# Attention scores on quarters of the TensorE array, with a PSUM bank per head

## The chip, the cores and the metric

The kernel runs on one core of one Trainium2 chip. A core has five engines that work on their own queues and wait for each other through semaphores: TensorE (PE in the profile; its weight loads are listed as PEld), VectorE (DVE), ScalarE (ACT), GpSimd (POOL) and SyncE (SP), which here issues nearly all DMA transfers. Matmuls write to PSUM, eight banks of 128 partitions by 512 fp32 words; everything else is in SBUF. The metric is the device time of one execution in microseconds (us). Before the change the median of three runs is 691.74 us (691.67 to 692.97).

## The reference

Two stages, all in fp32. The inputs q, k and v have 4 batches, 8 heads, 768 positions and 64 dimensions.

```python
k_sum = k.reshape(B, H, nb, 32, D).max(axis=3)          # nb = 24 summaries per head
v_sum = v.reshape(B, H, nb, 32, D).mean(axis=3)
scores_l = scale * q @ k.T                               # kept where |i - j| < 16
scores_s = scale * q @ k_sum.T + log(32)
a = softmax over [scores_l masked, scores_s]
attn = a @ [v, v_sum]                                    # (B, H, S, D)
x = attn.transpose(0, 2, 1, 3).reshape(B * S, H * D)     # 3072 x 512
h = x @ w_in                                             # 3072 x 2048
out = (h * erf(softplus(h))) @ w_out                     # 3072 x 512
```

So each query sees at most 31 neighbours and 24 summaries. The second stage, two large matrix products, is most of the arithmetic.

## The kernel before, in words

The work is cut into 12 chunks of 256 positions (3 per batch). In a chunk, attention is done in four "quads", one per pair of heads (`NP = 4`; quad number `qd = 4 * chunk + pair`), 48 in all. A quad has four blocks of 64 queries (`NB = 4`). The keys that a block can see are a window of 96, and with the 24 summaries each block has `NK = 120` columns of scores.

The scores of a quad (`scores`, L232 to L246) use a block diagonal. The tile `qb` holds, for each of the four blocks, a 128 x 128 matrix with the first head's queries in its upper left quarter and the second head's in its lower right; the other quarters are zero, cleared once by GpSimd (L57, L75). `load_quad` fills the two diagonal quarters with two transfers from `q_t` (L209). The keys of both heads lie one above the other on 128 partitions (`kw`, or `kfirst` and `ksum` for the first four quads). One matmul per block gives 128 rows (2 heads x 64 queries) by 120 columns, so four matmuls fill 480 columns of one PSUM bank. An fp32 matmul appears in the profile as two instructions.

What follows for a quad: `maxima` adds the mask out of PSUM (L254, DVE) and takes the row maximum (L257, L260); `exps` (L271, ACT); `weights_of` divides by the sum (DVE, L277 to L281); `transp` turns the weights, four PE transposes into PSUM (L291); `tcopy` copies them to SBUF as `pt` (L297, ACT); `av` multiplies by the values (L308, 8 matmuls of 64 output rows); `xsplit` takes the result out of PSUM as a high part xh and a rest xl (L326 or L328, and L329).

All these small PSUM results share the pool `ps_a`: two banks, taken in turn by `scores`, `transp`, `av` and the summaries' transpose (`summaries_turn`, L161). The hidden layer (`mm1`, L342) has the four banks of `ps_h` and the output (`mm2`, L395) the two of `ps_o`. The scores of the first four quads use a bank of `ps_h` each, and their q lies in `qbs` and `qfirst`.

The hidden layer goes in steps: 12 chunks by 4 groups of 512 hidden units, 48 steps k. Matrices are in a split form (a high and a low part, three passes) from the second chunk on; for the first chunk they are used in full fp32, and DVE puts each weight group together from raw words (`to32`, L106, L108, L110) while ACT and DVE then make the high and low parts (`high`, L127; `low`, L135).

The order of each engine's instructions is the order in which the program is written (`manual_schedule`); there is no planner. Up to step 3 the order is spelled out line by line (L446 to L611): this is the run-up. From k = 4 a loop (L613) does the same in each round: scores of quad k + 5, `mm1` first half, transposes of quad k + 4, `mm1` second half, `av` of quad k + 4, `mm2` of step k - 1. Steps 45 to 47 are written out again. Within a queue an instruction that waits holds up all that stands behind it.

Of the kernel before, what the change touches and what calls it, by code (L numbers as in the profile page):

```python
# [9 lines left out]
F32 = mybir.dt.float32  # L10
# [4 lines left out]
ALU = mybir.AluOpType  # L15
AX = mybir.AxisListType
PSUM = bass.MemoryType.PSUM
# [4 lines left out]
NP = H // 2  # L22
NTH = 3
NB = 4
NS = 24
LW = 96
NK = LW + NS
T = 256
# [12 lines left out]
def block_attention_mlp(ctx: ExitStack, tc: tile.TileContext, q_t, k_nat, k_win, v_tok, v_nat, v_win, w_in, w_out, out):  # L41
    nc = tc.nc

    const = ctx.enter_context(tc.tile_pool(name="const", bufs=1))
    wts = ctx.enter_context(tc.tile_pool(name="wts", bufs=1))
    two = ctx.enter_context(tc.tile_pool(name="two", bufs=2))
    one = ctx.enter_context(tc.tile_pool(name="one", bufs=1))
    small = ctx.enter_context(tc.tile_pool(name="small", bufs=2))
    ps_h = ctx.enter_context(tc.tile_pool(name="ps_h", bufs=4, space=PSUM))
    ps_o = ctx.enter_context(tc.tile_pool(name="ps_o", bufs=2, space=PSUM))  # L50
    ps_a = ctx.enter_context(tc.tile_pool(name="ps_a", bufs=2, space=PSUM))

# [7 lines left out]
    mask_sb = const.tile([128, 5, NK], F32, name="mask_sb")  # L60
    nc.gpsimd.memset(mask_sb[:, :, 0:LW], 0.0)
    nc.gpsimd.memset(mask_sb[:, :, LW:NK], 8.0 * math.log(32.0))
    for a in range(2):
        m = mask_sb[64 * a:64 * a + 64, :, 0:LW]
        nc.gpsimd.affine_select(out=m, in_=m, pattern=[[0, 5], [1, LW]], compare_op=ALU.is_ge, fill=-8e9, base=-1, channel_multiplier=-1)
        nc.gpsimd.affine_select(out=m, in_=m, pattern=[[0, 5], [-1, LW]], compare_op=ALU.is_ge, fill=-8e9, base=31, channel_multiplier=1)
    nc.gpsimd.memset(mask_sb[:, 0, 0:16], -8e9)
    nc.gpsimd.memset(mask_sb[:, 4, 80:LW], -8e9)
# [44 lines left out]
    def weave(*gens):  # L113

        gens = list(gens)
        while gens:
            for x in list(gens):
                if next(x, x) is x:
                    gens.remove(x)
# [37 lines left out]
        nc.vector.tensor_reduce(vs_sum[:, LW:NK], vn.rearrange("d (n w) -> d n w", n=NS), op=ALU.add, axis=AX.X)  # L157

    def summaries_turn(b, p):
        tp = ps_a.tile([128, 512], F32, name="pa")  # L160
        nc.tensor.transpose(tp[0:NK, 0:128], vs_sum, ident)  # L161
        nc.scalar.mul(vsum[b % 2][LW:NK, p], tp[LW:NK, 0:128], 1.0 / 32.0)

    kfirst = {}
# [36 lines left out]

    def load_quad(qd, values=True):
        ch, b, th, p = where(qd)
        qb = qbs[qd % 2] if qd not in qfirst else qfirst[qd]
        first = qd < NP
        kw = None if first else two.tile([128, NB, NK], F32, name="kw")
        for a in range(2):
            r = slice(64 * a, 64 * a + 64)
            nc.sync.dma_start(out=qb[r, :, r], in_=q_t[b, p, r, th * T:(th + 1) * T].rearrange("d (j q) -> d j q", j=NB))  # L209
# [12 lines left out]
    def ksum_quad(qd):  # L222
        ch, b, th, p = where(qd)
        s = st[qd]
        nc.gpsimd.tensor_copy(s["kw"][:, :, LW:NK], ksum[b % 2][:, p:p + 1, :].to_broadcast([128, NB, NS]))
# [4 lines left out]
        nc.sync.dma_start(out=s["vw"][LW:NK], in_=vsum[b % 2][LW:NK, p:p + 1, :].to_broadcast([NS, NB, 128]))  # L230

    def scores(qd):  # L232
        s = st[qd]
        sc = ps_h.tile([128, 512], F32, name="sf", tag="hps") if qd < NP else ps_a.tile([128, 512], F32, name="pa")
        for j in range(NB):
            if qd >= NP:
                parts = [(0, s["kw"][:, j])]
            else:

                kn, k0 = kfirst[qd], 64 * j - 16  # L240
                parts = [(0, kn[:, k0:k0 + LW])] if j else [(0, kn[:, 0:16]), (16, kn[:, 0:LW - 16])]
                parts.append((LW, ksum[0][:, qd]))
            for c, rhs in parts:
                c += j * NK
                nc.tensor.matmul(sc[:, c:c + rhs.shape[-1]], lhsT=s["qb"][:, j], rhs=rhs, start=True, stop=True)  # L245
        s["sc"] = sc  # L246

    def maxima(qd):
        ch, b, th, p = where(qd)
        s = st[qd]  # L250
        pr = wslot([128, NB, NK], F32, "prf") if qd < NP else two.tile([128, NB, NK], F32, name="pr")
        scv = s["sc"][:, 0:NB * NK].rearrange("q (j c) -> q j c", j=NB)
        mk = {0: mask_sb[:, 0:4], 1: mask_sb[:, 1:2].to_broadcast([128, NB, NK]), 2: mask_sb[:, 1:5]}[th]
        nc.vector.tensor_tensor(pr, scv, mk, op=ALU.add)  # L254
# [31 lines left out]

    def transp(qd):
        s = st[qd]
        tp = ps_a.tile([128, 512], F32, name="pa")
        for j in range(NB):  # L290
            nc.tensor.transpose(tp[0:NK, j * 128:(j + 1) * 128], s["pr"][:, j], ident)  # L291
        s["tp"] = tp

    def tcopy(qd):
        s = st[qd]
        pt = one.tile([NK, NB, 128], F32, name="pt")
        nc.scalar.copy(pt, s["tp"][0:NK].rearrange("c (j q) -> c j q", j=NB))  # L297
        s["pt"] = pt
# [2 lines left out]

    def av(qd):
        s = st[qd]
        xo = ps_a.tile([128, 512], F32, name="pa")
        for j in range(NB):
            for a in range(2):
                r = slice(64 * a, 64 * a + 64)
                nc.tensor.matmul(xo[r, j * 64:(j + 1) * 64], lhsT=s["vw"][:, j, r], rhs=s["pt"][:, j, r], start=True, stop=True)  # L308
        s["xo"] = xo[:, 0:T]

    def xsplit(qd):
        ch, b, th, p = where(qd)
        s = st.pop(qd)
        whole = ch == 0
        if p == 0:
            if whole:
                xt[ch] = [two.tile([128, NP, T], F32, name="xw", tag="xh")]
            else:
                xt[ch] = [two.tile([128, NP, T], F32R, name=n, tag=n) for n in ("xh", "xl")]
        xo = s["xo"]  # L320
        if whole:
            nc.scalar.copy(xt[ch][0][:, p], xo)
        else:
            xh, xl = (x[:, p] for x in xt[ch])
            if ch == 1:
                nc.scalar.copy(xh, xo)  # L326
            else:
                nc.vector.tensor_copy(xh, xo)  # L328
            nc.vector.tensor_tensor(xl, xo, f32(xh), op=ALU.subtract)  # L329
# [15 lines left out]
    wt = {}  # L345
# [195 lines left out]
    next(blocks)  # L541
    next(blocks)
# [70 lines left out]
    for k in range(4, NPER - 3):  # L613
# [41 lines left out]
        b, off = divmod(k, NTH * NG)  # L655
# [85 lines left out]
```

## Time and profile before

| what | value |
|---|---|
| median of three runs | 691.74 us |
| the profiled execution's own time | 695.52 us |
| its span, first to last instruction | 693.7 us |
| mean granted clock of TensorE | 0.985 |
| TensorE busy | 681.4 us, 98% |
| VectorE busy | 383.0 us, 55% |
| ScalarE busy | 421.4 us, 61% |
| chain that ended last, on TensorE | 93% |
| scores in the `pa` banks, share of that chain | 5% |

The profile is of one execution. Durations of matmuls overlap, since the array is a pipeline; the distance from start to start tells what one costs. The timeline lists the start and duration of instructions, then engine, line, operation, and the tiles written and read. "Idle before" names what an engine waited for. The chain of waits goes back from the last instruction to whatever released each step.

### The profile page before, as it was taken

To read this page: it belongs to the slowest core of one execution; us is meant where nothing else is said; L and a number is where in the kernel's file an instruction comes from. 1 tells how busy PE (TensorE), PEld (TensorE's weight loads), DVE (VectorE), ACT (ScalarE), POOL (GpSimd) and SP (SyncE) were. 2 spreads that over 40 slices of the span, in tenths; PEclk is the share of its full clock that TensorE was granted. 3 is DMA by queue.
4 is the path that set the end of the run, shared out by engine and by line. 5 is a ranking of instruction groups with operands and counts; after the bars stand their busy time and mean duration, and the time that the engine had idled before them with its cause. 6 is when DMAs were issued, how large, how long until landed. Compare 5 with 4: busy or idle time off the path is not lost.

```text
span 693.7 us, 12117 instructions
## 1 busy us (share of the span) xinstructions
PE 681.4 (98%) x4818; PEld 600.6 (87%) x4818; DVE 383.0 (55%) x741; ACT 421.4 (61%) x792; POOL 22.4 (3%) x67
## 2 busy tenths in 40 slices
PE   5999999999999999999999999999999999999997
PEld 4986677899889989988998998899889989989996
DVE  4489997987445444656544454565545444544132
ACT  2365777975664665566556655755765665565562
POOL 3000100000000000000000000000000000000000
PEclk8599999999999999999999999999999999999999
DMA  8995742422320322433311211343221131010000
GB/s 202 336 328 188 265 148 68 139 82 85 100 62 16 89 59 75 135 92 86 89 37 51 89 37 44 117 134 101 79 61 37 54 86 37 35 48 1 32 1 30
DMA packets 57895, 65.14 MB, mean 94 GB/s; under 512 B 29296, under 2 KB 42736, under 8 KB 57840
## 3 DMA queue, kind: packets, MB, share of 16 engines
q1 hardware_dynamic: 57552, 64.11, 30.9%
q8 instruction: 38, 0.62, 0.4%
q10 hardware_dynamic: 288, 0.26, 0.1%
q14 instruction: 17, 0.14, 0.1%
HBM read 55.90 MB, written 6.29 MB: 90 GB/s over the span
## 4 chain that ended last, share of the span: by engine, by line
PE 93%; DMA 2%; ACT 2%; DVE 1%; POOL 0%; issue 0%; SPq 0%; POOLq 0%
PE hps L342 40%; PE ops L395 38%; PE pa L245 5%; PE pa L308 4%; PE pa L291 3%; PE ops L189 1%; PE sf L245 1%; DMA kf<-k_nat 1%; DMA vf<-v_tok 1%; DVE tb L108 0%; DMA kw<-k_win 0%; SPq L209 0%; ACT ho L127 0%; DVE tb L106 0%; ACT pt L297 0%
## 5 line engine op out<-in xcount | busy, mean ns | idle before, releaser
L342 PE MATMUL hps<-xh,hi 128*128 128x256 f32 x704 | 205.7, 292 | 0.0
L342 PE MATMUL hps<-xl,hi 128*128 128x256 f32 x704 | 199.2, 283 | 0.0
L342 PE MATMUL hps<-xh,li 128*128 128x256 f32 x704 | 199.2, 283 | 0.0
L350 ACT ACTIVATE wt<-hps 128x512 f32<-128x512 f32 x96 | 57.2, 597 | 217.3 <-PE hps L342 216.1
L395 PE MATMUL ops<-ho,gh 128*128 128x512 f32 x336 | 136.9, 407 | 0.0
L342 PEld LDWEIGHTS hps<-xl,hi 128*128 128x128 f32 x704 | 135.0, 192 | 0.2
L342 PEld LDWEIGHTS hps<-xh,hi 128*128 128x128 f32 x704 | 134.8, 191 | 0.2
L342 PEld LDWEIGHTS hps<-xh,li 128*128 128x128 f32 x704 | 134.7, 191 | 0.0
L395 PE MATMUL ops<-ho,gl 128*128 128x512 f32 x336 | 133.2, 396 | 0.0
L395 PE MATMUL ops<-lo,gh 128*128 128x512 f32 x336 | 133.1, 396 | 0.0
L395 PEld LDWEIGHTS ops<-ho,gh 128*128 128x128 f32 x336 | 63.3, 188 | 15.9
L395 PEld LDWEIGHTS ops<-lo,gh 128*128 128x128 f32 x336 | 63.3, 188 | 14.8
L377 DVE TENSOR_TENSOR wt<-wt,hps 128x512 f32<-128x512 f32 x88 | 56.4, 681 | 34.0 <-ACT wt L365 34.0
L395 PEld LDWEIGHTS ops<-ho,gl 128*128 128x128 f32 x336 | 63.4, 189 | 13.4
L254 DVE TENSOR_TENSOR pr<-pa,mask_sb 128x480 f32<-128x480 f32 x44 | 28.9, 656 | 78.9 <-PE pa L245 78.9
L271 ACT ACTIVATE pr<-pr,mx 128x120 f32<-128x120 f32 x176 | 67.4, 385 | 4.0 <-DVE mx L260 3.5
L415 ACT ACT_TABLE_LOAD x49 | 62.9, 1283 | 1.6 <-PEq L734 0.7
L416 ACT ACT_TABLE_LOAD x49 | 62.9, 1283 | 0.9
L328 DVE CAST xh<-pa 128x256 fp32r<-128x256 f32 x40 | 17.0, 425 | 83.7 <-PE pa L308 83.7
L361 ACT ACTIVATE wt<-wt,half_b 128x1024 f32<-128x1024 f32 (+1 forms) x49 | 54.8, 1120 | 0.1
L383 DVE TENSOR_TENSOR gl<-wt,gh 128x512 fp32r<-128x512 f32 x84 | 54.1, 685 | 0.0
L277 DVE TENSOR_SCALAR rs<-sm 128x4 f32<-128x4 f32 x48 | 8.1, 169 | 79.0 <-ACT pr L271 76.3
(90 smaller groups left out, 807.3 us busy)
## 6 DMA issues: line engine op xcount, KB each, us to landing
kw<-k_win SPq DMA_DIRECT2D x44, 240.0 KB
vw<-v_win SPq DMA_DIRECT2D x44, 192.0 KB
rw<-w_in SPq DMA_DIRECT2D x8, 1024.0 KB
rw<-w_out SPq DMA_DIRECT2D x8, 1024.0 KB
qb<-q_t SPq DMA_DIRECT2D x92, 64.0 KB
out<-ob SPq DMA_DIRECT2D x22, 256.0 KB
kn<-k_nat SPq DMA_DIRECT2D x12, 384.0 KB
vn<-v_nat SPq DMA_DIRECT2D x12, 384.0 KB
```

The lines of the kernel that those rows point to most:

```text
L245: nc.tensor.matmul(sc[:, c:c + rhs.shape[-1]], lhsT=s["qb"][:, j], rhs=rhs, start=True, stop=True)
L254: nc.vector.tensor_tensor(pr, scv, mk, op=ALU.add)
L271: nc.scalar.activation(s["pr"][:, j], s["pr"][:, j], AF.Exp, scale=0.125, bias=s["nm"][:, j:j + 1], accum_out=sm[:, j:j + 1])
L308: nc.tensor.matmul(xo[r, j * 64:(j + 1) * 64], lhsT=s["vw"][:, j, r], rhs=s["pt"][:, j, r], start=True, stop=True)
L342: nc.tensor.matmul(hs[k, half][:, i], lhsT=w, rhs=xt[ch][x][:, cc], start=(cc == 0 and i == 0 and n == 0), stop=(cc == 3 and i == 1 and n ...
L350: nc.scalar.activation(wt[k][:, 2 * half:2 * half + 2], hs[k, half], AF.Tanh, scale=0.5)
L361: nc.scalar.activation(w, w, AF.Ln, scale=-0.49999994, bias=half_b)
L377: nc.vector.tensor_tensor(gh[:, s] if whole else w[:, s], w[:, s], hs.pop((k, n)), op=ALU.mult)
L383: nc.vector.tensor_tensor(gs[k][1][:, s], w[:, s], f32(gh[:, s]), op=ALU.subtract)
L395: nc.tensor.matmul(os_[ch][t], lhsT=x[m][:, i, q], rhs=w, start=(g == 0 and i == 0 and n == 0), stop=(g == NG - 1 and i == G - 1 and n == ...
L415: log_set = lambda: nc.scalar.preload_act_table_set("natural_log_exp_and_others")
L416: erf_set = lambda: nc.scalar.preload_act_table_set("sigmoid_and_others")
```

## The change

The scores are no longer taken from a block diagonal. For each block and each head there is one matmul of its own: 64 rows (the head's dimensions) by 64 queries as weights, 120 columns of keys. It reads the partitions of its head (0 to 63 or 64 to 127) and writes the partitions of its block's parity, so that the four combinations fall on the four quarters of the array. A quad has 8 such matmuls (18 for a quad of the first four, whose keys come in parts) in place of 4 (or 9). The two heads write to two different banks; a bank then holds two blocks side by side on each half of the partitions.

With that go: `ps_a` becomes one tile `pab` of two fixed banks. `scores` writes both, `transp` uses bank 0, `av` and `summaries_turn` use bank 1. The first four quads take two banks of `ps_h` each. `qb` is a plain [128, 256] tile, four buffers, one transfer per quad; the cleared tiles are gone. The mask gets a form per chunk position, built with 12 selections on GpSimd in place of 4. `maxima` reads both banks in one instruction, or in two for the first four quads. `av` picks its columns by the new layout. In the run-up, `av` and `xsplit` of a quad are put ahead of the next `scores` at three places, since these need both banks.

```diff
-    ps_a = ctx.enter_context(tc.tile_pool(name="ps_a", bufs=2, space=PSUM))
+    ps_a = ctx.enter_context(tc.tile_pool(name="ps_a", bufs=1, space=PSUM))
...
-    qbs = [const.tile([128, NB, 128], F32, name=f"qb{i}") for i in range(2)]
-    for t in qbs:
-        nc.gpsimd.memset(t, 0.0)
...
+    pab = ps_a.tile([128, 2, 512], F32, name="pa")
...
+    for c in range(2):
+        for th in range(NTH):
+            m = mask_sb[64 * c:64 * c + 64, th, :, 0:LW]
+            nc.gpsimd.affine_select(out=m, in_=m, pattern=[[0, 2], [1, LW]], compare_op=ALU.is_ge, fill=-8e9, base=-1, channel_multiplier=-1)
+            nc.gpsimd.affine_select(out=m, in_=m, pattern=[[0, 2], [-1, LW]], compare_op=ALU.is_ge, fill=-8e9, base=31, channel_multiplier=1)
...
-    qfirst = {p: two.tile([128, NB, 128], F32, name="qf", tag="wt") for p in (2, 3)}
-    for t in qfirst.values():
-        nc.gpsimd.memset(t, 0.0)
...
     def load_quad(qd, values=True):
-        qb = qbs[qd % 2] if qd not in qfirst else qfirst[qd]
+        qb = two.tile([128, T], F32, name="qb", tag="qb", bufs=4)
...
-        for a in range(2):
-            r = slice(64 * a, 64 * a + 64)
-            nc.sync.dma_start(out=qb[r, :, r], in_=q_t[b, p, r, th * T:(th + 1) * T].rearrange("d (j q) -> d j q", j=NB))
+        nc.sync.dma_start(out=qb, in_=q_t[b, p, :, th * T:(th + 1) * T])
...
     def scores(qd):
+        s = st[qd]
+        sc = [pab[:, a] for a in range(2)] if qd >= NP else [ps_h.tile([128, 512], F32, name="sf", tag="hps") for _ in range(2)]
+        for i in range(2):
+            for c in range(2):
+                j = 2 * i + c
+                for a in range(2):
+                    r, o = slice(64 * a, 64 * a + 64), slice(64 * c, 64 * c + 64)
+                    if qd >= NP:
+                        parts = [(0, s["kw"][r, j])]
...
+                    for n, rhs in parts:
+                        n += i * NK
+                        nc.tensor.matmul(sc[a][o, n:n + rhs.shape[-1]], lhsT=s["qb"][r, 64 * j:64 * j + 64], rhs=rhs, start=True, stop=True)
...
     def maxima(qd):
...
+        if qd >= NP:
+            nc.vector.tensor_tensor(prv, pab[:, :, 0:2 * NK], mk.to_broadcast([128, 2, 2 * NK]), op=ALU.add)
+        else:
+            for a in range(2):
+                nc.vector.tensor_tensor(prv[:, a], s["sc"][a][:, 0:2 * NK], mk[:, 0], op=ALU.add)
...
     def transp(qd):
-        tp = ps_a.tile([128, 512], F32, name="pa")
+        tp = pab[:, 0]
...
     def av(qd):
-        xo = ps_a.tile([128, 512], F32, name="pa")
+        xo = pab[:, 1]
...
     mm2(0, (0, 1))
     transp(NP)
     tcopy(NP)
+    av(NP)
+    xsplit(NP)
     ksum_quad(NP + 2)
     scores(NP + 2)
-    av(NP)
...
     weave(weights_of(NP + 1), maxima(NP + 2))
-    xsplit(NP)
...
     gsplit(1)
+    xsplit(NP + 1)
     scores(NP + 3)
     load_quad(NP + 4, False)
-    xsplit(NP + 1)
...
     high("i", 1)
-    scores(NP + 4)
     load_quad(NP + 5)
     to32_half("o", 2, 0)
     av(NP + 3)
+    xsplit(NP + 3)
+    scores(NP + 4)
     weave(to32("o", 2, 1), maxima(NP + 4))
-    xsplit(NP + 3)
```

More of the change, by code (lines that the diff above doesn't have):

```diff
@@ L50, in block_attention_mlp @@
     ps_o = ctx.enter_context(tc.tile_pool(name="ps_o", bufs=2, space=PSUM))
-    ps_a = ctx.enter_context(tc.tile_pool(name="ps_a", bufs=2, space=PSUM))
+    ps_a = ctx.enter_context(tc.tile_pool(name="ps_a", bufs=1, space=PSUM))
     ident = const.tile([128, 128], F32, name="ident")
     make_identity(nc, ident)
-    qbs = [const.tile([128, NB, 128], F32, name=f"qb{i}") for i in range(2)]
-    for t in qbs:
-        nc.gpsimd.memset(t, 0.0)
-    mask_sb = const.tile([128, 5, NK], F32, name="mask_sb")
-    nc.gpsimd.memset(mask_sb[:, :, 0:LW], 0.0)
-    nc.gpsimd.memset(mask_sb[:, :, LW:NK], 8.0 * math.log(32.0))
-    for a in range(2):
[L64 to L68, printed above, removed]
+    pab = ps_a.tile([128, 2, 512], F32, name="pa")
+    mask_sb = const.tile([128, NTH, 2, NK], F32, name="mask_sb")
+    nc.gpsimd.memset(mask_sb[:, :, :, 0:LW], 0.0)
+    nc.gpsimd.memset(mask_sb[:, :, :, LW:NK], 8.0 * math.log(32.0))
+    for c in range(2):
[3 more added lines that the diff above has]
+            nc.gpsimd.affine_select(out=m, in_=m, pattern=[[0, 2], [-1, LW]], compare_op=ALU.is_ge, fill=-8e9, base=31, channel_multiplier=1)
+    nc.gpsimd.memset(mask_sb[0:64, 0, 0, 0:16], -8e9)
+    nc.gpsimd.memset(mask_sb[64:128, 2, 1, 80:LW], -8e9)
     vs_sum = const.tile([128, NK], F32, name="vs_sum")
@@ L159, in summaries_turn @@
     def summaries_turn(b, p):
-        tp = ps_a.tile([128, 512], F32, name="pa")
+        tp = pab[:, 1]
         nc.tensor.transpose(tp[0:NK, 0:128], vs_sum, ident)
@@ L233, in scores @@
         s = st[qd]
[L234 to L245, printed above, removed]
+        sc = [pab[:, a] for a in range(2)] if qd >= NP else [ps_h.tile([128, 512], F32, name="sf", tag="hps") for _ in range(2)]
[7 more added lines that the diff above has]
+                    else:
+                        kn, k0 = kfirst[qd], 64 * j - 16
+                        parts = [(0, kn[r, k0:k0 + LW])] if j else [(0, kn[r, 0:16]), (16, kn[r, 0:LW - 16])]
+                        parts.append((LW, ksum[0][r, qd]))
+                    for n, rhs in parts:
+                        n += i * NK
+                        nc.tensor.matmul(sc[a][o, n:n + rhs.shape[-1]], lhsT=s["qb"][r, 64 * j:64 * j + 64], rhs=rhs, start=True, stop=True)
         s["sc"] = sc
@@ L307, in av @@
                 r = slice(64 * a, 64 * a + 64)
-                nc.tensor.matmul(xo[r, j * 64:(j + 1) * 64], lhsT=s["vw"][:, j, r], rhs=s["pt"][:, j, r], start=True, stop=True)
+                nc.tensor.matmul(xo[r, j * 64:(j + 1) * 64], lhsT=s["vw"][:, j, r], rhs=s["pt"][:, 2 * a + j // 2, 64 * (j % 2):64 * (j % 2) + 64], start=True, stop=True)
         s["xo"] = xo[:, 0:T]
```

8 lines of the change are left out of this document (3 added, 5 removed).

## The prediction

> **What bounds the kernel now.** The page comes first: the span, the engines' shares and the granted clock in 40 slices. Then the groups of instructions, for the line that the change rewrites.
>
> ```profile
> span 693.7 us, 12117 instructions
> PE 681.4 (98%) x4818; PEld 600.6 (87%) x4818; DVE 383.0 (55%) x741; ACT 421.4 (61%) x792; POOL 22.4 (3%) x67
> PEclk8599999999999999999999999999999999999999
> L245 PE MATMUL pa<-kw,qb 128*128 128x120 f32 x352 | 46.3, 275 | 0.1
> ```
>
> TensorE (PE) is busy for 98% of the span, and over all 44 score blocks in the `pa` banks it waited 0.1 us. So what a score block takes from PE's queue it takes from the time, and a new wait of PE is paid in full. The clock row matters too: the second slice (17 to 35 us) runs mostly at half clock.
>
> One round of the long loop, in order of time; columns are start, duration, engine, line, instruction:
>
> ```profile
> 302.19 0.40 PE L395 MATMUL ops<-lo,gh 128*128 128x512 f32 x1
> 302.42 1.05 PE L245 MATMUL pa<-kw,qb 128*128 128x120 f32 x8
> 303.23 0.36 PE L342 MATMUL hps<-xh,hi 128*128 128x256 f32 x1
> 303.43 0.28 PE L342 MATMUL hps<-xl,hi 128*128 128x256 f32 x1
> 303.55 0.28 PE L342 MATMUL hps<-xh,li 128*128 128x256 f32 x1
> ...
> 306.19 0.60 PE L291 MATMUL pa<-ident,pr 128*120 128x128 f32 x4
> 306.62 0.27 PE L161 MATMUL pa<-ident,vs_sum 128*120 128x128 f32 x1
> ...
> 309.49 0.28 PE L342 MATMUL hps<-xh,li 128*128 128x256 f32 x1
> 309.70 0.69 PE L308 MATMUL pa<-pt,vw 120*64 120x64 f32 x16
> 310.31 0.50 PE L395 MATMUL ops<-ho,gh 128*128 128x512 f32 x1
> 310.64 0.40 PE L395 MATMUL ops<-ho,gl 128*128 128x512 f32 x1
> 310.88 0.40 PE L395 MATMUL ops<-lo,gh 128*128 128x512 f32 x1
> ...
> 316.01 1.05 PE L245 MATMUL pa<-kw,qb 128*128 128x120 f32 x8
> ```
>
> The same view cut off inside the L308 block, after 6 and after 14 of its 16 instructions, and two rows of VectorE (DVE):
>
> ```profile
> 309.70 0.39 PE L308 MATMUL pa<-pt,vw 120*64 120x64 f32 x6
> ...
> 309.70 0.63 PE L308 MATMUL pa<-pt,vw 120*64 120x64 f32 x14
> ...
> 303.50 0.66 DVE L254 TENSOR_TENSOR pr<-pa,mask_sb 128x480 f32<-128x480 f32 x1 [0.93 <-PE pa L245]
> ...
> 310.89 0.42 DVE L329 TENSOR_TENSOR xl<-pa,xh 128x256 fp32r<-128x256 f32 x1
> ```
>
> Durations overlap in the pipeline, so I count starts. From the last output matmul before the scores (302.19) to the second matmul after them (303.43) pass 1.24 us. Without scores those are one output step (310.64 to 310.88: 0.24) and one hidden-layer step (303.43 to 303.55: 0.12). **A score block now costs 1.24 - 0.36 = 0.88 us**: 8 instructions (each fp32 matmul is two) at 0.11.
>
> **The new score block.** It has 8 matmuls of 64x64 with the same 120 moving columns, so 16 instructions, on four quarters. If the four quarters run side by side, each does 2 matmuls, 4 instructions. The nearest row is L308, which already works on two halves of the array (120*64). Its 6th to 14th instruction add 0.63 - 0.39 = 0.24 us: 0.03 each, 0.06 per pair. One stream of 64 columns alone should take 0.054 (the four transposes at L291 stream 128 columns in about 0.43/4 = 0.108 us, to 306.62 where the next matmul starts). So two halves do run at once, and their weight loads are hidden. For 120 columns that gives 0.101 to 0.11 per step, and 4 steps make 0.42.
>
> To this comes the change of the array's division. L308 costs 310.64 - 309.49 - 0.12 - 0.24 = 0.79 us, of which 8 pairs are 0.47; the other 0.32 is what stands around it: 0.21 instead of 0.12 before it, 0.15 between its last start and the next, and 0.33 instead of 0.24 after. The old score block shows next to none of that. A new block is then 0.42 + 0.32 = 0.74, **0.14 us less, 44 times: -6.2 us**. Bounds: if the switch costs 0.25, -0.21 each (-9.2); if row halves of the array do not overlap as column halves do, 8 steps, 0.84 + 0.32 = 1.16, +0.28 each (+12.3). I take the value nearest to L308's row, the only divided array in the trace.
>
> The Trainium skill (TensorE: Matmul & The Clock Gate, Part 3, "The mechanism") says that weight loads overlap running matmuls only when the row group differs, which speaks against this change, since two quarters share each row half. L308's two halves share all rows, and their pairs still take 0.06 where streaming alone takes 0.054, so the trace does not agree. The same part ("Measured speedup vs the span model") gives a set of tiles one matmul's time plus about 4 ns a tile; by that the body would be 0.45 in place of 0.42, an estimate.
>
> **The shared banks in the loop.** `pab` is now one pair of banks in place of a rotation of two. Scores need both, so they wait for the xl subtraction (L329), which ends at 311.31, 4.7 us before 316.01. The transposes wait for the mask add (L254), which ends at 304.16, 2.0 us before 306.19. Both are covered by the matmuls between, and cost nothing.
>
> **The shared banks in the run-up.** There the order written out has less between them. The rows of four places:
>
> ```profile
> 58.66 0.62 PE L291 MATMUL pa<-ident,pr 128*120 128x128 f32 x4 [0.42 <-DVE pr L281]
> 59.12 1.05 PE L245 MATMUL pa<-kw,qb 128*128 128x120 f32 x8
> 60.12 0.69 PE L308 MATMUL pa<-pt,vw 120*64 120x64 f32 x16
> ...
> 72.33 1.15 PE L245 MATMUL pa<-kw,qb 128*128 128x120 f32 x8
> ...
> 82.02 3.72 PE L342 MATMUL hps<-xw,wi 128*128 128x256 f32 x16 [0.38 <-DVE wi L110]
> ...
> 89.47 1.05 PE L245 MATMUL pa<-kw,qb 128*128 128x120 f32 x8
> ...
> 101.80 0.60 PE L291 MATMUL pa<-ident,pr 128*120 128x128 f32 x4
> ```
>
> The same places on ScalarE (ACT) and DVE, and DVE's busy time over the stretch (columns of the last row: stretch, length, PE, PEld, DVE, ACT, POOL, clock, DMA, GB/s):
>
> ```profile
> 59.50 0.56 ACT L297 COPY pt<-pa 120x512 f32<-120x512 f32 x1
> ...
> 92.05 0.37 ACT L326 CAST xh<-pa 128x256 fp32r<-128x256 f32 x1
> ...
> 60.41 1.22 DVE L110 SCALAR_TENSOR_TENSOR wi<-rw,tb 128x1024 uint32<-128x1024 uint32 x1
> ...
> 72.85 0.42 DVE L329 TENSOR_TENSOR xl<-pa,xh 128x256 fp32r<-128x256 f32 x1 [0.16 <-ACT xh L326]
> ...
> 102.72 0.65 DVE L254 TENSOR_TENSOR pr<-pa,mask_sb 128x480 f32<-128x480 f32 x1
> ...
> 60.00:105.00 45.00, 44.62 (x258) 31.93 (x256) 42.60 (x64) 29.55 (x55) 3.84 (x4) 1.00 0.59 196
> ```
>
> A, quad NP+2 (59 us). Today its scores fill the time in which ACT copies `pt` (to 60.06). Now av(NP) comes first: PE idles from 59.12 to 60.12 (1.0), does av to about 60.73, then waits for xsplit: DVE is in the weight conversion until 61.63, then subtracts (0.42), so scores start near 62.05 (1.3 more). **+2.25**. Behind them in PE's queue stand mm2(0,(2,3)) and mm1(2), and DVE's next mask add.
> B, quad NP+3. Its scores now wait for xl, 72.85 + 0.42 = 73.27, instead of starting at 72.33: **+1.0**. Of A and B, about 0.4 is given back at 82.02, where PE waits for DVE's `wi` today.
> C, quad NP+4. av(NP+3) now goes at 89.47 and ends near 90.2, but ACT's xh stands behind high("i",1) and ends at 92.42; xl and then scores follow at about 93.0: **+2.85**, with mm2(2) queued behind. DVE's add and everything after it in its queue move as much.
> D, k = 4. The transposes at 101.80 now need bank 0, which L254 reads until 103.37: **+1.6**.
> Sum **+7.3 us**. Bounds: 4 (DVE and ACT get there earlier than their order suggests) to 9 (A and C each lose another 0.8, since DVE is busy for 42.60 of these 45 us and cannot catch up).
>
> **The start.** Rows of the chain of waits (start, duration), the wait table (total, times, longest), the SP queue and a stretch:
>
> ```profile
> 16.38 4.01 PE sf L245 x18
> ...
> 23.96 3.67 PE sf L245 x18
> ...
> PE sf L245 <- DMA vf<-v_tok: 5.4, 1, 5.4
> ...
> 1.44 1.39 SPq L209 DMA_DIRECT2D qb<-q_t x2
> ...
> 7.09 2.97 SPq L209 DMA_DIRECT2D qf<-q_t x4
> ...
> 16.40:32.20 15.80, 15.80 (x85) 15.63 (x86) 7.94 (x16) 4.09 (x16) 0.00 (x0) 0.50 1.06 346
> ```
>
> PE waits 5.4 us for the third quad's loads (scores(2) reads kf, ksum and qf, so I read the `vf` of that row as the q transfers that share its queue), and then works 15.8 us without a gap at clock 0.50. Each q load is now one transfer of 1 KB rows without a cleared tile ahead of it: SP spends half of its 1.39 us on the first, saves as much on the second, and reaches the third quad's last transfer some 2.2 us earlier; with a quarter of the packets I take 3 us for scores(2). Its duration falls as well: 36 instructions in four quarters, 10 at most in one, at half clock 0.12 to 0.17 each, 1.3, and twice 0.32 around it: 2.0 in place of 4.0 and 3.7, with less gained where the transposes' inputs come late; 3.7 together. So about 6.7 us of half-clock time are won. If the clock comes back at the same moment, this is worth half, 3.4; if it follows the denser work, all of it. **-5.0 us**, bounds -1.5 and -7.
>
> Costed at nothing: more mask pieces on POOL less four memsets (hidden by those 5.4 us), two half-size adds for the first four quads instead of one, and one q issue in place of two in the loop, where PE waits for no transfer.
>
> **Sum.** -6.2 + 7.3 - 5.0 = -3.9 us. The profiled execution took 695.52 us (span 693.7), the median is 691.74; the saving goes through unscaled: **687.8**, own range 683.5 to 691.
>
> **Rivals.**
> 1. The full clock comes back later (slower). Place: 16 to 40 us. PE was busy for all of the 15.80 us at 0.50, so being busy is not enough, and the new score blocks keep fewer instructions in the array. At 32 us the start is 3.4 us ahead; every further us at half clock costs 0.5. From 4.6 us later on the change is slower, and 7 us later the start's gain is gone: 691.74 - 6.2 + 7.3 = 692.8; twice as late, 696. Against: what ran just before the clock came back is unchanged and comes earlier.
> 2. The row halves do not overlap: 691.74 + 12.3 + 7.3 - 3 = 708. For: no row of this trace divides the rows. Against: nothing in it but the likeness to the column halves.
> 3. Weight loads of the two quarters that share a row half do not hide. The body is then 4 steps of 0.101 + 0.054, 0.62, the block 0.94, +0.06 each, +2.6: 691.74 + 2.6 + 7.3 - 4.5 = 697.1. L308's pairs speak against it. This is the rule of the Trainium skill's page named above.
> 4. The run-up loses only 4 and the start wins 7: 691.74 - 6.2 + 4 - 7 = 682.5.
>
> **Chances.** Forecast 0.50, rival 1 0.15, rival 2 0.08, rival 3 0.09, rival 4 0.18. Under 0.2% (1.4 us) this measurement cannot tell a change from none. Faster: the forecast but for its edge, and rival 4: 0.65. Same: that edge and half of rival 1: 0.10. Slower: rivals 2 and 3 and the rest of 1: 0.25. The range 681 to 697 leaves out rival 2, half of rival 3 and a little below.
>
> **What would show it.** The block in the loop: 16 L245-type records on 64*64 in some 0.74 us between output and hidden matmuls, four starting together; by rival 2 1.16, by rival 3 0.94. The loop's round shorter by 0.14. In the waits, PE's scores on DVE xl some 1 to 3 us at three places before 100 us, and the transposes once on the mask add. At the start, the wait of 5.4 ending near 13, and the half clock over before or at 32 us. Waits of PE in the long loop would make the prediction wrong, as would a gap between quarters.

## The result, and the profile after

The change makes the kernel slower: 703.34 us (median of 4 runs, 702.69 to 705.88), against 692.36 (691.67 to 693.09) for the kernel before on the same chip, a ratio of 1.0165 [1.0136, 1.0195]. The forecast was 687.8 with a range up to 697.

The page of the kernel after: span, shares and granted clock. TensorE's share has gone from 98% to 96%, and the sixth slice of the clock row (88 to 106 us) shows 8, where the row before shows 9 from the third slice on.

```profile
span 703.9 us, 12980 instructions
PE 674.6 (96%) x5242; PEld 568.4 (81%) x5242; DVE 383.6 (54%) x745; ACT 421.5 (60%) x792; POOL 20.8 (3%) x71
PEclk9899989999999999999999999999999999999999
```

The wait table of TensorE after (total, times, longest):

```profile
PE pa L158 <- ACT pt L301: 8.7, 12, 0.7
PE pa L245 <- issue: 5.0, 3, 2.7
PE sf L245 <- DMA qb<-q_t: 4.1, 1, 4.1
...
PE pa L312 <- ACT pt L301: 0.8, 1, 0.8
```

Its first line is new, has twelve entries, and stands in the long loop, which had no waits before: L158 is the summaries' transpose (L161 before the change). The timeline of one such round, PE and then ACT:

```profile
308.80 0.39 PE L399 MATMUL ops<-lo,gh 128*128 128x512 f32 x1
309.12 0.64 PE L245 MATMUL pa<-kw,qb 64*64 64x120 f32 x16
309.69 0.39 PE L346 MATMUL hps<-xh,hi 128*128 128x256 f32 x1
309.91 0.28 PE L346 MATMUL hps<-xl,hi 128*128 128x256 f32 x1
...
312.67 0.60 PE L295 MATMUL pa<-ident,pr 128*120 128x128 f32 x4
314.00 0.32 PE L158 MATMUL pa<-ident,vs_sum 128*120 128x128 f32 x1 [0.73 <-ACT pt L301]
```

```profile
313.36 0.58 ACT L301 COPY pt<-pa 120x512 f32<-120x512 f32 x1
```

The summaries' transpose no longer follows the four transposes at once (before: 306.19, then 306.62). It starts at 314.00, after ScalarE has copied their result (313.36 to 313.94). The copy reads bank 0 and the summaries' transpose writes bank 1, but both are halves of one tile.

By bank there was nothing to wait for: the last reader of bank 1, the mask add of this round, ran from 309.82 to 310.48.

The same score block as in the timeline, with the view ending after its first 4, 8 and 12 instructions:

```profile
309.12 0.33 PE L245 MATMUL pa<-kw,qb 64*64 64x120 f32 x4
...
309.12 0.44 PE L245 MATMUL pa<-kw,qb 64*64 64x120 f32 x8
...
309.12 0.54 PE L245 MATMUL pa<-kw,qb 64*64 64x120 f32 x12
```

Four instructions are a step of 0.10 to 0.11 us (0.33, 0.44, 0.54, and 0.64 for all 16): all four quarters run together. From 308.80 to 309.91 is 1.11, less the 0.36 of two whole-array steps: the block costs 0.75.

Where the time went, from the two profiled executions (693.7 and 703.9 us of span). The marks are the starts of the score blocks of quads 4 and 10 in the timelines: 45.45 and 112.78 before, 40.19 and 116.75 after. Each is one execution; their own times, 695.52 and 705.88 us, both lie above the medians.

| stretch | before | after | difference |
|---|---|---|---|
| start, to quad 4 | 45.45 | 40.19 | -5.3 |
| run-up, quad 4 to quad 10 | 67.33 | 76.56 | +9.2 |
| loop and end, from quad 10 | 580.9 | 587.1 | +6.2 |

In the loop a round without summaries takes 13.35 us, before 13.48; a round with summaries 14.40, before 13.59. So a score block saves 0.13, and the new wait costs 0.81 + 0.13 = 0.94 in each of 12 rounds: **11.3 us** (the 0.73 of the wait, and the pipeline that runs empty and fills again).

In the run-up, the chain of waits after the change (start, duration) and the clock of its parts (columns: stretch, length, PE, PEld, DVE, ACT, POOL, clock, DMA, GB/s):

```profile
54.12 0.48 ACT pt L301
54.60 0.04 issue
54.64 0.69 PE pa L312 x16
55.33 1.26 issue
56.59 0.98 PE pa L245 x16
57.57 4.94 PE ops L399 x8
...
70.47 0.98 issue
71.45 0.64 PE pa L245 x16
72.09 3.63 PE ops L399 x8
```

```profile
56.80:60.20 3.40, 3.40 (x20) 1.57 (x12) 2.58 (x6) 0.50 (x3) 0.11 (x1) 0.51 0.83 237
...
88.80:90.80 2.00, 0.00 (x0) 0.00 (x0) 0.00 (x0) 2.00 (x3) 0.27 (x1) 1.00 0.69 212
90.90:97.70 6.80, 6.21 (x22) 2.92 (x23) 6.03 (x9) 4.54 (x11) 0.72 (x1) 0.50 0.25 65
```

Stall A is the 0.84 us before the av block at 54.64 (the wait table's L312) and the 1.26 of "issue" before the scores; B is the 0.98 before 71.45; C is a wait of 2.73 before the scores at 91.49, with PE empty in the second stretch of the clock rows. The profile names no releaser for the scores, but in each place they start 0.1 us after the subtraction that reads bank 1 has ended (56.50, 71.35 and 91.38):

```profile
56.08 0.42 DVE L333 TENSOR_TENSOR xl<-pa,xh 128x256 fp32r<-128x256 f32 x1
...
70.92 0.43 DVE L333 TENSOR_TENSOR xl<-pa,xh 128x256 fp32r<-128x256 f32 x1 [0.16 <-ACT xh L330]
...
90.96 0.42 DVE L333 TENSOR_TENSOR xl<-pa,xh 128x256 fp32r<-128x256 f32 x1 [3.20 <-ACT xh L330]
```

What the forecast did not have is the clock: behind A it is 0.5 for 3.4 us and behind C for 6.8 us. Eight output matmuls take 4.94 at 57.57, and eight others of the same shape 3.63 at 72.09.

### The profile page after: what moved, and what is told of

Read it like the earlier page. It is cut to its first block, busy times and chain, and to the rows that moved or that the text cites. A ratio compares the mean times of both kernels' runs of the same rounds, so it can differ in the third digit from the quotient of the medians.

```text
span 703.9 us, 12980 instructions
## 1 busy us (share of the span) xinstructions
PE 674.6 (96%) x5242; PEld 568.4 (81%) x5242; DVE 383.6 (54%) x745; ACT 421.5 (60%) x792; POOL 20.8 (3%) x71
## 4 chain that ended last, share of the span: by engine, by line
PE 88%; ACT 4%; DMA 3%; DVE 2%; issue 2%; SPq 1%; POOL 0%; ACTq 0%; POOLq 0%
PE hps L346 39%; PE ops L399 39%; PE pa L312 4%; PE pa L245 4%; PE pa L295 2%; DMA rw<-w_in 2%; ACT pt L301 1%; DMA kw<-k_win 1%; ACT pr L275 1%; PE ops L186 1%; PE pa L158 1%; SPq L204 0%; ACT L419 0%; DVE lo L132 0%; SPq L214 0%
## 5 line engine op out<-in xcount | busy, mean ns | idle before, releaser
L369 ACT ACTIVATE wt<-wt 128x1024 f32<-128x1024 f32 (+1 forms) x49 | 50.9, 1041 | 0.5
## 6 DMA issues: line engine op xcount, KB each, us to landing
rw<-w_in SPq DMA_DIRECT2D x8, 1024.0 KB, 11.1
```

Of the source, the lines that this page charges most:

```text
L369: nc.scalar.activation(w, w, AF.Erf, scale=-1.0)
```

## The experiments

All times are medians; each ratio is to runs of the kernel before that were made beside it (692.2 to 692.4 each time). "Quad 4" and "quad 10" are read from one profiled execution each, as above, so the last three columns need not add up to the medians.

| kernel | us | ratio [interval] | quad 4 at | quad 4 to 10 | from quad 10 |
|---|---|---|---|---|---|
| before | 692.36 | 1 | 45.45 | 67.33 | 580.9 |
| after | 703.34 | 1.0165 [1.0136, 1.0195] | 40.19 | 76.56 | 587.1 |
| two tiles | 688.26 | 0.9947 [0.9925, 0.9969] | 35.50 | 76.46 | 575.6 |
| summaries later | 692.24 | 0.9999 [0.9980, 1.0018] | 38.27 | 76.66 | 575.7 |
| two tiles, filled stalls | 688.02 | 0.9935 [0.9917, 0.9953] | 38.88 | 73.20 | 575.6 |
| before, banks in one tile | 708.56 | 1.0226 [1.0196, 1.0257] | 44.32 | 71.48 | 592.3 |
| two tiles, split visit | 703.81 | 1.0164 [1.0141, 1.0187] | 36.39 | 76.69 | 588.8 |
| two tiles, q in pieces | 692.07 | 0.9991 [0.9972, 1.0010] | 41.58 | 75.24 | 576.3 |
| two tiles, new order | 686.85 | 0.9917 [0.9896, 0.9938] | 38.80 | 72.31 | 575.6 |
| one tile, new order, summaries later | 687.02 | 0.9925 [0.9903, 0.9947] | 36.83 | 72.42 | 575.8 |
| hybrid | 683.81 | 0.9878 [0.9853, 0.9903] | 37.70 | 68.76 | 576.2 |
| two tiles, new order, less VectorE | 683.92 | 0.9865 [0.9838, 0.9893] | 39.58 | 68.06 | 575.6 |

### Two tiles

```diff
-    pab = ps_a.tile([128, 2, 512], F32, name="pa")
+    pab = [ps_a.tile([128, 512], F32, name=f"pa{i}") for i in range(2)]
...
-        if qd >= NP:
-            nc.vector.tensor_tensor(prv, pab[:, :, 0:2 * NK], mk.to_broadcast([128, 2, 2 * NK]), op=ALU.add)
-        else:
-            for a in range(2):
-                nc.vector.tensor_tensor(prv[:, a], s["sc"][a][:, 0:2 * NK], mk[:, 0], op=ALU.add)
+        for a in range(2):
+            nc.vector.tensor_tensor(prv[:, a], s["sc"][a][:, 0:2 * NK], mk[:, 0], op=ALU.add)
...
```

> The changed kernel, with the pair of banks as two tiles and the mask add in two halves. Theory: in 12 rounds the summaries' transpose (bank 1) waits for ACT's copy out of bank 0, since the pair is one tile and is tracked as a whole; a round with it takes 14.40 instead of 13.35 + 0.11, so 0.94 each, 11.3 in all. With two tiles this wait is gone: 703.3 - 11.3 = 692.0, rounds of 13.46 where a summary is turned. Rival: the loss comes from the divided array or from the transposes themselves, or the copy must come first for another reason: 703 and the wait of 0.73 stays.

Measured 688.26 us. The wait at L158 is gone; the transposes and the summaries' transpose stand together again:

```profile
303.00 0.60 PE L292 MATMUL pa<-ident,pr 128*120 128x128 f32 x4
303.43 0.27 PE L158 MATMUL pa<-ident,vs_sum 128*120 128x128 f32 x1
```

Rounds with summaries take 13.46. From quad 10 to the end the kernel takes 575.6 us, 11.5 less than the kernel after and 5.3 less than the kernel before. The wait in the loop belongs to the single tile. The whole is 3.7 us below the expectation, and in the profile this lies ahead of quad 4 (35.50 instead of 40.19).

### Summaries later

The single tile stays; the summaries' transpose moves into the middle of the second half of the hidden layer, by when the copy is done.

```diff
-        if nb + 1 < B and 6 <= off < 10:
-            summaries_turn(nb + 1, off - 6)
...
-        mm1(k, 1)
+        mm1(k, 1, (0, 1))
+        if nb + 1 < B and 6 <= off < 10:
+            summaries_turn(nb + 1, off - 6)
+        mm1(k, 1, (2, 3))
         tanh(k, 1)
```

> The changed kernel, with the summaries' transpose put into the middle of the second half of the hidden layer, 1.4 us later in PE's queue. Theory: the copy out of bank 0 has ended by then, so PE does not wait: 692.0, as with two tiles. Rival: av needs bank 1 and now waits for ACT's copy of the summary behind the second tanh: part of the 11.3 comes back, 695 to 700.

Measured 692.24, the expected 692.0: the one wait was 11.1 us. The kernel before measured the same 692.24 beside it. The loop's gain and the start's are eaten by the run-up (76.66 against 67.33).

The two ways to remove the wait differ by 4.0 us, though rounds and run-up are the same. In the profiles 2.8 of the 3.0 us between them lie before quad 4, where the one ran 3.4 us at half clock and the other 10.2. The other executions go the same way: over ten of each the granted clock is 0.992 with two tiles and 0.988 here, which by an estimate from these two numbers is 5 us more at half clock, worth up to 2.5 us. Whether the single tile causes this is open: in the new order of the run-up, below, one tile and two are equal.

### The kernel before with its two banks in one tile

Block diagonals, everything as before; only the two banks of `ps_a`, used in the same turn, are halves of one tile.

```diff
-    ps_a = ctx.enter_context(tc.tile_pool(name="ps_a", bufs=2, space=PSUM))
+    ps_a = ctx.enter_context(tc.tile_pool(name="ps_a", bufs=1, space=PSUM))
...
+    pair = ps_a.tile([128, 2, 512], F32, name="pa")
+    turn = []
+    def bank():
+        turn.append(0)
+        return pair[:, len(turn) % 2]
...
```

> The kernel before, with block diagonals, only that its two banks are one tile whose halves are used in turn as before. Theory: the wait belongs to the single tile and not to the quarters: 12 rounds lose 0.94, and quad 6's scores wait for the copy in the run-up (1.0): 692.4 + 12.3 = 704.7. Rival: the quarters make the wait: 692.4.

Measured 708.56. The wait table of this kernel, whose summaries' transpose is L168:

```profile
PE pa L168 <- ACT pt L304: 8.7, 12, 0.7
...
PE pa L298 <- DVE pr L261: 1.4, 1, 1.4
PE ops L402 <- DVE wo L117: 1.0, 1, 1.0
PE pa L252 <- issue: 0.9, 1, 0.9
```

The same twelve waits with the same 8.7 us appear without any quarter of the array. A round with summaries takes 14.52 to 14.64, 13.59 without the single tile. The run-up loses 4.2 us too, with waits of the transposes, a weight part and the scores (the other three rows) that the kernel before does not show, and so the sum is 3.9 above the expectation.

### Filled stalls

Two tiles, and 24 matmuls of zeros into a free bank ahead of the stalls A (3 and 5), B (4) and C (12). They compute nothing that is used.

```diff
+    def fill(n, bank):
+        for _ in range(n):
+            nc.tensor.matmul(pab[bank], lhsT=zeros[:, 0:128], rhs=zeros, start=True, stop=True)
...
     tcopy(NP)
+    fill(3, 1)
     av(NP)
     xsplit(NP)
+    fill(5, 0)
...
```

> Two tiles as in e1, and 24 matmuls on zeros whose results are overwritten, put where PE stands still in the run-up (3 and 5 at quad 6, 4 at quad 7, 12 at quad 8). Theory: the granted clock falls to 0.5 at 57 and 91 us because PE idles 1 to 2.7 us there, which costs 1.3 + 2.6 = 3.9; with the gaps filled it stays at 1.00 from 30 us on: 692.0 - 3.9 = 688.1, the gaps themselves stay. Rival: the small score blocks or the wait for DMA near there set the clock: 692, clock 0.5 in the same places.

The clock, from 29 us to the scores of quad 10, and for comparison two stretches of the kernel with two tiles:

```profile
29.00:112.08 83.08, 80.06 (x505) 52.97 (x506) 69.56 (x105) 53.56 (x103) 8.63 (x7) 1.00 0.64 217
```

```profile
51.20:58.00 6.80, 6.14 (x20) 2.88 (x21) 5.63 (x12) 2.66 (x9) 1.29 (x1) 0.50 0.88 301
...
88.70:92.10 3.40, 3.40 (x5) 1.34 (x6) 3.35 (x5) 1.97 (x2) 0.66 (x1) 0.51 0.29 80
```

In the profile the clock stays full with the stalls filled, and the stretch from quad 4 to quad 10 takes 73.20 instead of 76.46: there the half clock behind the stalls costs 3.3 us (forecast 3.9). The medians do not show it, 688.02 against 688.26. That 688.1 was expected is luck, since it was counted from 692.0. One reason can be read from the runs: the half clock behind the stalls is not in every execution. Six of the ten executions of the kernel with two tiles had a granted clock of 0.993 to 0.998, so by an estimate from these numbers (2 x 0.007 x 687) at most 9.6 us at half clock in all, less than the 10.2 us that the profiled one had in the run-up alone.

### Split visit

The score block in two halves, with 12 hidden matmuls between them, in each of 39 rounds.

```diff
+    def scores(qd, halves=range(2)):
...
+        for i in halves:
...
-            scores(qs)
+            scores(qs, (0,))
+            mm1(k, 0, (0,))
+            scores(qs, (1,))
             if k > 4:
                 rowmax(qs)
-        mm1(k, 0)
+            mm1(k, 0, (1, 2, 3))
+        else:
+            mm1(k, 0)
```

> The kernel with two tiles, and in the long loop the 16 instructions of a score block go in two visits of 8, with the first quarter of the hidden layer's half step (12 hidden matmuls) between them: 39 visits more, not one score matmul more. My theory (a visit to the divided array costs about 0.32 us whatever it does, the rest of a block is 4 steps of about 0.10): each of the 39 rounds is 0.25 to 0.35 us longer, the round without summaries about 13.65 instead of 13.35, and the whole 688.3 + 39 x 0.3 = 700 us (698 to 702). Rival (no price of a visit; the block of 0.74 is the matmuls themselves at 0.18 a step): rounds as before, 688.3 us. A second rival (the loss at a visit is only the latency of the first and the last matmul, which overlaps whole-array matmuls): between, under 0.1 a visit, below 692 us.

```profile
305.10 0.39 PE L396 MATMUL ops<-lo,gh 128*128 128x512 f32 x1
305.42 0.43 PE L245 MATMUL pa<-kw,qb 64*64 64x120 f32 x8
305.79 0.39 PE L343 MATMUL hps<-xh,hi 128*128 128x256 f32 x1
...
306.48 0.28 PE L343 MATMUL hps<-xh,li 128*128 128x256 f32 x1
306.69 0.44 PE L245 MATMUL pa<-kw,qb 64*64 64x120 f32 x8
307.06 0.39 PE L343 MATMUL hps<-xh,hi 128*128 128x256 f32 x1
```

A round without summaries takes 13.70 instead of 13.35: a visit costs 0.34 to 0.35 us beside its matmuls, and from quad 10 on the kernel is 13.2 us longer. Both rivals fall by this (nothing, or under 0.1). Half a block takes 0.37 from its start to the next matmul's, for two steps of 0.10. The forecast's 0.32, taken from the av block, holds nearly. The whole, 703.81, misses the expected 698 to 702: the medians differ by 15.6, and in the profiles 1.1 us of this lies ahead of quad 10.

### q in pieces

Two tiles, with q loaded as before the change: two transfers a quad, in pieces of 256 bytes. The matmuls are the same.

```diff
-        qb = two.tile([128, T], F32, name="qb", tag="qb", bufs=4)
+        qb = two.tile([128, NB, 72], F32, name="qb", tag="qb", bufs=4)
...
-        nc.sync.dma_start(out=qb, in_=q_t[b, p, :, th * T:(th + 1) * T])
+        for a in range(2):
+            r = slice(64 * a, 64 * a + 64)
+            nc.sync.dma_start(out=qb[r, :, 0:64], in_=q_t[b, p, r, th * T:(th + 1) * T].rearrange("d (j q) -> d j q", j=NB))
```

> The kernel with two tiles, with q loaded as before the change, by two transfers of 256-byte pieces a quad, into a tile with gaps; the score matmuls are the same. Theory (the start's gain comes half from the transfers: the third quad's q lands about 3 us earlier with one transfer of 1 KB rows): the third quad's scores start about 2 to 3 us later than in the kernel with two tiles, the whole is 1.5 to 3 us longer, 690 to 691 us. Rival (the gain is all from the shorter score blocks of the first four quads and where the half clock falls): the third quad's scores start within 0.5 us, 688.3 us.

The third quad's first scores with two tiles, and with q in pieces:

```profile
12.25 0.56 PE L245 MATMUL sf<-kf,qb 64*64 64x16 f32 x9 [3.39 <-DVE mx L258]
```

```profile
15.06 0.77 PE L247 MATMUL sf<-kf,qb 64*64 64x16 f32 x6 [5.91 <-DVE rs L280]
```

They start 2.8 us later, as expected, and the whole is 692.07 instead of 688.26: 3.8 us, more than the expected 1.5 to 3. (With two tiles this quad's q is issued at 4.77 and takes 7.4 us to land, so it is the load that came last, and not the engine that the row names.) The 2.8 us are the transfers. The 3.8 us of the whole are theirs only in part as far as is shown: the two kernels above with the same loads differ by 4.0, and the granted clock of the ten executions is 0.990 here and 0.992 with two tiles. With q as before, quad 4 still starts 3.9 us ahead of the kernel before (41.58 against 45.45); the shorter score blocks and less half clock are left for that.

### A new order in the run-up

Two tiles, and output matmuls that stood behind the scores are put into the stalls; at C the high parts move behind the split on ScalarE.

```diff
     tcopy(NP)
+    mm2(0, (2,))
     av(NP)
     xsplit(NP)
     ksum_quad(NP + 2)
+    mm2(0, (3,))
     scores(NP + 2)
...
-    mm2(0, (2, 3))
...
     xsplit(NP + 1)
+    mm2(1, (0,), (0,))
     scores(NP + 3)
...
-    mm2(1, (0, 1))
+    mm2(1, (0,), (1,))
+    mm2(1, (1,))
...
-    high("i", 1)
     load_quad(NP + 5)
     to32_half("o", 2, 0)
     av(NP + 3)
     xsplit(NP + 3)
+    high("i", 1)
+    mm2(2, (0,))
     scores(NP + 4)
...
-    mm2(2, (0, 1))
+    mm2(2, (1,))
```

> The kernel with two tiles, and in the run-up output matmuls that stood behind the scores are put ahead of them at the three places of stalls A, B and C (one output group ahead of av of quad 4 and one ahead of the scores of quad 6; half of one ahead of the scores of quad 7; one ahead of the scores of quad 8, with the high parts of a weight group moved behind the split of quad 7 on ScalarE). Theory (these stalls cost 5.8 us of waiting and 3.9 us by the half clock that follows them): the stretch from the scores of quad 4 to those of quad 10 takes 68 to 70 us instead of 76.5, the clock stays full after 30 us, and the whole takes 688.3 - 5.8 - 3.9 + 1 = 680 us (678 to 683). Rival (VectorE, busy for 42.6 of 45 us there, is the bound of the run-up): the waits come back a few us later at the weight parts, and the whole stays at 685 to 688 us.

Measured 686.85: the rival's range. The clock is full and the waits A, B and C are gone, but the stretch takes 72.31 and not 68 to 70. The wait table of PE and the stretch:

```profile
PE ops L396 <- DVE wo L107: 2.3, 2, 1.8
PE hps L343 <- DVE wi L107: 1.6, 2, 1.2
...
PE ops L396 <- DVE gh L378: 0.9, 2, 0.5
PE pa L292 <- DVE pr L255: 0.9, 1, 0.9
```

```profile
38.80:111.11 72.31, 66.15 (x406) 42.48 (x405) 62.61 (x98) 48.59 (x93) 7.45 (x6) 1.00 0.62 206
```

New waits name VectorE. The single tile with the same order and the later summaries gives the same:

> The same new order in the run-up, on the kernel with one tile whose summaries' transposes stand in the middle of the hidden layer's second half. Theory: 8 us or more below that kernel's 692.2, so 681 to 685 us; what it keeps over the two tiles is only the start. Rival: one tile costs more in the run-up than two, since there every reader of one bank holds up the writers of the other: 686 to 690 us.

Measured 687.02, stretch 72.42; its expectation of 681 to 685 falls with that of the two tiles. The number lies in its rival's range, but not for the rival's reason: one tile costs no more here than two (72.31).

### Less work for VectorE

The new order, without the second of three instructions that put together each half of a weight group from the second group on (the weights' lowest bits are missing).

```diff
-        nc.vector.scalar_tensor_tensor(tb, rw[..., 0], 29, tb, op0=ALU.logical_shift_right, op1=ALU.bitwise_or)
+        if g == 0:
+            nc.vector.scalar_tensor_tensor(tb, rw[..., 0], 29, tb, op0=ALU.logical_shift_right, op1=ALU.bitwise_or)
```

> The new run-up order on two tiles, and VectorE leaves out the second of the three instructions that put together each half of a weight group, from the second group on (1.2 us each, so the lowest bits of these weights are missing): some 9 us less VectorE work between the scores of quad 4 and quad 10. Theory (with the new order VectorE bounds the run-up): the stretch falls from 72.3 to 66 to 68 us, the whole from 686.9 to 681 to 683. Rival (the weights' transfers or TensorE's own order bound it): the stretch stays within 1 us of 72.3 and the whole at 686 to 687.

```profile
39.58:107.64 68.06, 65.75 (x406) 42.51 (x405) 51.45 (x88) 48.37 (x93) 2.80 (x6) 1.00 0.61 211
```

With 11.2 us less VectorE work the stretch falls by 4.25 to 68.06, just above the expected 66 to 68, and PE is busy for 65.75 of it. So with the new order VectorE's queue was what held up the run-up, right behind the stalls. The whole, 683.92, is 1 us above the expected 681 to 683.

### The hybrid

Quarters everywhere but for quads 6, 7 and 8, which keep the block diagonal in one bank, and the order of before at their places. The two banks are taken in turn.

```diff
+    OLD = (NP + 2, NP + 3, NP + 4)
...
     def scores(qd):
         s = st[qd]
+        if qd in OLD:
+            s["sc"] = bank()
+            for j in range(NB):
+                nc.tensor.matmul(s["sc"][:, j * NK:(j + 1) * NK], lhsT=s["qb"][:, j], rhs=s["kw"][:, j], start=True, stop=True)
+            return
+        sc = [bank(), bank()] if qd >= NP else [ps_h.tile([128, 512], F32, name="sf", tag="hps") for _ in range(2)]
...
```

> Quarters for the first four quads, for quads 4 and 5 and for all of the long loop; block diagonals of one bank, as before the change, for quads 6, 7 and 8 alone, whose places were stalls A, B and C, and there the order of before. The two banks are taken in turn again, so a score block on quarters takes both and every other result one. Theory (the run-up loses because a score block needs both banks): from the scores of quad 4 to those of quad 10 takes 67 to 68.5 us, as before the change, instead of 76.5; quad 4 keeps its start of 36 to 39 us, so quad 10 comes at 104 to 106 and the whole takes 679 to 682 us. Rival (VectorE has 62 us of work in this stretch in every kernel, and the weight words that it puts together are no earlier): what the start gained is lost again behind VectorE, the stretch takes 71 to 73 us, the whole 685 to 687.

Measured 683.81, 0.9878 [0.9853, 0.9903] of the kernel before: the lowest time of the kernels that do all the work, and clear of both the kernel before and the kernel after. The run-up takes 68.76, 0.3 above the expected 67 to 68.5, and the whole lies between the theory's range and the rival's.

```profile
37.70:106.46 68.76, 65.90 (x382) 44.53 (x381) 62.49 (x96) 48.57 (x93) 4.16 (x6) 1.00 0.66 214
```

```profile
95.35 0.63 PE L319 MATMUL pa<-ident,pr 128*120 128x128 f32 x4 [1.45 <-DVE pr L282]
```

Up to quad 9 the timeline keeps the distances of the kernel before (52.49 from quad 4, before 52.58). What is left is stall D: the transposes of quad 8 wait 1.45 us for the mask add of quad 9, whose scores are on quarters and took both banks.

## Why the prediction was wrong

**The score block: right.** Forecast 0.88 to 0.74; measured 0.75, and 0.13 a round. Body and price of a visit are as forecast (steps of 0.10; 0.34 to 0.35 for 0.32). Rivals 2 and 3 fall with the three rows that end after 4, 8 and 12 instructions: row halves overlap, and the loads of quarters that share a row half are hidden. The rule of the Trainium skill (TensorE: Matmul & The Clock Gate, Part 3, "The mechanism") that the prediction cites does not agree with these rows: by rival 3, an estimate that follows it, each step would have been 0.155. What the 0.34 of a visit consists of, no run separates.

**The start: right in size, in part by luck.** -5.3 us in the two profiles, forecast -5.0. The third quad's scores start 4.0 us earlier (12.35, before 16.38), of which 2.8 are the q transfers by the kernel with q in pieces; the forecast had put 3. The rest is not a fixed gain: in nine profiles with the new loads quad 4 starts at 35.5 to 40.2 us, at 35.5 with 3.4 us of half clock ahead of it, at 36.4 to 38.8 with 6.8 and at 38.3 to 40.2 with 10.2. The kernel before varies too: its profiled execution had 20.5 us of half clock at the start and a granted clock of 0.985, while 27 of the 52 on record beside the experiments stood at 0.993 or more, so its start is not always as late as 45.45. Rival 1 did not come as put: the last half clock of the start ended at 29.4, before at 32.2.

**The shared banks in the loop: wrong, and this is the step that failed.** The prediction said that scores and transposes are covered by the matmuls between "and cost nothing". That holds for the two that it looked at; PE waits at neither in the loop. It passed over the third user of the banks, the summaries' transpose, though its row stood in the prediction's own fence at 306.62, directly behind the transposes. It also counted waits by bank, and by bank this transpose was free; the wait goes by tile. With nothing between them it waits for the copy of the transposes' result, 12 times 0.94 us: 11.3 of the 15.5 us by which the forecast was off. (The run-up, below, makes 2.8 more; 0.6 is that the kernel before measured 692.36 and not 691.74.) Two tiles remove it, a later place removes it, and the kernel before gets it when its banks are put into one tile.

**The shared banks in the run-up: three places right, the sum too small.** A, B and C came as forecast (2.10 for 2.25, 0.98 for 1.0, 2.73 for 2.85). D did not occur in the kernel after, where TensorE came later than the mask add; it came in the hybrid, 1.45 for 1.6. But the stretch lost 9.2 us where 7.3 less some 0.8 for its six blocks was forecast. The term left out is the half clock behind A and C, 3.3 us by the filled stalls in the profiled executions, though by the granted clocks not in every execution. With the single tile made two, the kernel takes 688.26, beside the forecast's 687.8, but by luck: in its profile the start wins 10.0 and the run-up loses 9.1, where 5.0 and 6.5 were forecast.

**Rival 4** gave 682.5 for a run-up that loses little; the hybrid, which takes its scores off the stalls, comes to 683.81.

Open is what part of the 4 us between the two kernels without the wait in the loop is not the clock, and what decides how much half clock falls at the start.

## What to carry to other kernels

When buffers that rotated become one tile, list every user of that tile, also those that run in only some rounds, and ask for each who last read or wrote any part of it: here the wait was between two halves that never touch the same bank. Small matmuls on quarters do run side by side, but a visit to the divided array costs what it costs, here nearly half of the block; gather such work into few visits. A stall in a tight order written by hand can be paid twice, once as the wait and once more in the clock behind it, and when it is filled another engine may stand right behind as the bound. Whether it is paid twice can differ from one execution to the next, so compare the granted clocks before you put a few us between two kernels down to their code.

## What the runs showed of the hardware

In the kernel after, waits of 0.84 and 1.26 us within 3 us were enough for 3.4 us of half clock, and one of 2.73 for 6.8 us; with two tiles the first place got 6.8 and the second 3.4 (rows above), so the wait alone does not set the length. In the profiles of all twelve kernels each stretch of half clock ahead of quad 10 lasted 3.41 us or a multiple of it, up to 20.5. In the kernel after these stretches begin at 12.38, 22.62, 56.75 and 90.88, which lie 3, 10 and 10 times 3.41 us apart: in these profiles the clock changes on a fixed grid. So what a stall costs may depend on how it falls on the grid, which no run here tests. In the grid step ahead of 56.75 PE was busy for 1.31 of 3.41 us, ahead of 90.88 for 1.29; with the new order a step with 1.60 (from 88.64) brought no half clock, but with two tiles one with 1.98 (from 47.80) did, so no threshold comes out of these runs. At half clock PE was busy all along at the first place (3.40 of 3.40 us at 56.80). The Trainium skill (TensorE: Matmul & The Clock Gate, Part 1) has the clock go down after an idle window of about 3.4 us; no single wait before these places is that long, so the runs agree with the length of the window but not with one that is idle throughout.

Four quarters of the array run together, and from step to step (0.10 us) their weight loads cost nothing, even of two that share their rows. A visit to the divided array costs 0.34 to 0.35 us beside its matmuls.
